# A two-stage transformer block on one core: who writes the 64 duplicated columns of the normalised x in the first chunk

## The chip, the cores and the metric

The kernel runs on one core of a Trainium2 chip. A core has five engines that run side by side, each with its own instruction queue: TensorE (PE in the profile, with its weight loads as PEld), VectorE (DVE), ScalarE (ACT), GpSimd (POOL) and SyncE (SP), which here only starts DMA transfers. An instruction starts when those ahead of it on its engine have started and every semaphore that it waits for has been reached. The metric is the time of one execution in microseconds (us), as the median of several runs.

## The reference, cut to what matters

x has 2048 rows of 576 columns. It is normalised row by row, and the normalised rows feed two branches, whose product is added to x:

```python
xn = _layernorm(x, axis=-1)          # (x - mean) / sqrt(var + 1e-5)
s = _A_ref(xn, A_wqkv, A_wo)         # 32 heads of 18, causal window of 256, softmax, output projection
g = _silu(_B_ref(xn, w_gate, w_up, w_down))   # (sigmoid(xn @ w_gate) * (xn @ w_up)) @ w_down, F = 4608
return x + s * g
```

All tensors are bf16. By far the most work is in the three 576 x 4608 products.

## The kernel before

The rows are worked on in four chunks of 512 (NC = 4, BPC = 4 blocks of 128 rows in each). For each chunk the kernel normalises x, brings it into transposed form (`xnT`, columns of x along the partitions), makes q, k and v, does the windowed attention, the output projection, the gate and up products (instruction names `f1`), their combination `hT`, and the down product (`f2`). All matmuls use 64 rows of the array, two at a time: one on rows 0 to 63 and one on rows 64 to 127. 576 columns are 64 + 4 x 128, so the first 64 columns of x are a block of their own, and both halves of the array need that block. That is why a normalised block `xnr` has 640 columns: columns 64 to 639 hold the 576 normalised values, and columns 0 to 63 are a second copy of the first 64 of them (RD = 64, XW = 640).

The normalisation of block i is built in `build_ln`. For blocks 0, 1 and 3 of the first chunk: two `bn_stats` on VectorE (L545, L547), `bn_aggr` (L549), variance plus epsilon (L551), the power -1/2 on GpSimd (L553), then the normalisation of 576 columns on VectorE (L561, name `ln:ap`), and a copy of 64 columns on VectorE (L565, `ln:dup`). Block 2 has its sums from ScalarE instead (`STATS_ACT = (2,)`): L604 sums x, GpSimd turns that into the negative mean (L605), L606 sums squares, GpSimd makes variance (L607) and the power (L608). Then the same L561 and L565 follow. In the first chunk TensorE transposes the 640 columns of each block in ten pieces of 64 x 64 (L617, `tr`), and ScalarE (blocks 0 to 2) or VectorE (block 3) copies the result from PSUM to `xnT` (L594, `xe`). In later chunks a DMA transposes; there L561 and L565 stay as they are.

Before the first block is ready TensorE has nothing to do, and 106 "warm" matmuls on zeros stand there (L131 with `hT` as input): 86 ahead of the first transposes and 20 behind them. After that come the gate and up products of the first two groups of 128 hidden columns, cut into four parts of 128 rows, so that part i can start as soon as block i is in `xnT` (`NEARLY = 2`, `PARTS`).

The order of the instructions on every engine is not the order of the code. `build_graph` makes a list of operations with their dependencies and an estimated duration (`op(engine, ns, ...)`), `schedule` simulates the engines with those estimates and always takes the operation that can start first, and `emit` writes each engine's list with the semaphore waits. So a changed estimate or a changed engine can move operations on all engines. Small buffers are rings (`Ring`): the statistics have three slots (`NST = 3`), so the statistics of block 3 go where those of block 0 were and wait until their last reader is done; the normalised blocks have two (`NXN = 2`), so block 2 waits for the transposes of block 0.

Of the kernel before, what the change touches and what calls it, by code (L numbers as in the profile page):

```python
# [4 lines left out]
ACTF = mybir.ActivationFunctionType  # L5
ALU = mybir.AluOpType
# [8 lines left out]
RD = 64  # L15
# [59 lines left out]
REM_PRIO = 0.6  # L75
STATS_ACT = (2,)
APPLY_ACT = ()
DUP_ACT = ()
XE_ENG = ("ACT", "ACT", "ACT", "DVE")
NWARM = (43, 10)  # L80
NEARLY = 2
# [25 lines left out]
def act_ns(n):  # L107
    return n / 1.2 + 175.0
# [34 lines left out]
def dve_ns(n, rate=1.0):  # L143
    return n / (0.96 * rate) + 160.0
# [118 lines left out]
class Builder:  # L263
# [17 lines left out]
    def op(self, eng, est, fn, name="", deps=(), prio=3, nbytes=0, odeps=(), acq=None, ni=0):  # L281
        o = Op(eng, est, fn, name, deps, prio, nbytes, odeps, acq)
        o.ni = ni
        assert ni or eng != "PE", name
        o.cidx = len(self.ops)
        self.ops.append(o)
        for d in o.deps:
            d.succs.append(o)
        for d in o.odeps:
            d.succs.append(o)  # L290
        return o
# [237 lines left out]
    def build_ln(self, c):  # L529
        op = self.op  # L530
        xs = c % 2
        war = self.xnT_rel[c - 2] if c >= 2 else []
        for i in range(BPC):
            st = c * BPC + i
            if c and i % 2 == 0:
                self.load_x(c, i)
            pr = 2 if c else LN_PRIO[i]
            o_x, x_in = self.x_dma[st]
            ss, ds = self.r_st.produce()
            on_act = c == 0 and i in STATS_ACT  # L540
            if on_act:
                mean, rs = self.act_stats(x_in, o_x, pr)
                ag = None
            else:
                b1 = op("DVE", 390, lambda e, ss=ss, x_in=x_in: e.bn_stats(self.bnst[:, ss, 0, :], x_in[:, 0:288]),  # L545
                        f"ln:bn1:{st}", deps=[o_x, ds], prio=pr)
                b2 = op("DVE", 390, lambda e, ss=ss, x_in=x_in: e.bn_stats(self.bnst[:, ss, 1, :], x_in[:, 288:576]),  # L547
                        f"ln:bn2:{st}", deps=[o_x, ds], prio=pr)
                ag = op("DVE", 200, lambda e, ss=ss: e.bn_aggr(self.mv[:, ss, :], self.bnst[:, ss, :, :]),  # L549
                        f"ln:ag:{st}", deps=[b1, b2], prio=pr)  # L550
                ve = op("DVE", 140, lambda e, ss=ss: e.tensor_scalar(self.veps[:, ss, :], self.mv[:, ss, 1:2], EPS, None,  # L551
                                                                    ALU.add), f"ln:ve:{st}", deps=[ag], prio=pr)
                rs = op("POOL", 560, lambda e, ss=ss: e.tensor_tensor(self.rstd[:, ss, :], self.veps[:, ss, :],  # L553
                                                                      self.neghalf[:, :], ALU.pow),
                        f"ln:rs:{st}", deps=[ve, self.op_negh], prio=pr)
                mean = self.mv[:, ss, 0:1]
            rstd = self.arstd[:, :] if on_act else self.rstd[:, ss, :]
            sn, dn = self.xn_slot[st] if c else self.r_xn.produce()

            def norm(e, mean=mean, rstd=rstd, x_in=x_in, sn=sn, op0=ALU.add if on_act else ALU.subtract):  # L560
                return e.tensor_scalar(self.xnr[:, sn, RD:XW], x_in, mean, rstd, op0, ALU.mult)  # L561

            def f_dup(e, sn=sn):
                dst, sr = self.xnr[:, sn, 0:RD], self.xnr[:, sn, RD:2 * RD]
                return e.activation(dst, sr, ACTF.Copy) if e is self.nc.scalar else e.tensor_copy(dst, sr)  # L565
            if c == 0 and i in APPLY_ACT:
                nb = op("DVE", 150, lambda e, mean=mean, rstd=rstd, sg=1.0 if on_act else -1.0: e.tensor_scalar(
                    self.nbias[:, :], mean, rstd, sg, ALU.mult, ALU.mult), f"ln:nb:{st}", deps=[rs, ag], prio=pr)
                ap = op("ACT", act_ns(D), lambda e, rstd=rstd, x_in=x_in, sn=sn: e.activation(
                    self.xnr[:, sn, RD:XW], x_in, ACTF.Identity, bias=self.nbias[:, :], scale=rstd), f"ln:ap:{st}", deps=[nb, dn], prio=pr)  # L570
            else:
                ap = op("DVE", 430, norm, f"ln:ap:{st}", deps=[rs, ag, dn], prio=pr)
            dup_act = c == 0 and i in DUP_ACT
            dup = op("ACT" if dup_act else "DVE", act_ns(RD) if dup_act else 180, f_dup, f"ln:dup:{st}", deps=[ap], prio=pr)
            self.ln_dup = dup
            self.r_st.release(ss, ap)
            if c:
                fl = self.flip(self.xnT[:, xs, :, i * P:(i + 1) * P], self.xnr[:, sn, :], f"flip:x:{st}", ("fx", xs, i),
                               deps=[dup, war], prio=2)
                self.r_xn.release(sn, fl)  # L580
                self.op_xnT[c].append(fl)
                continue
            h = self.pool_s.hold()

            def f_tr(eng, h=h, sn=sn):
                return self.transposes(eng, h, lambda r, o: self.xnr[r, sn, o:o + P])
            tr = op("PE", KB * 29.5, f_tr, f"tr:{st}", deps=[ap, dup, self.op_ident, war], prio=0, acq=h, ni=20)
            self.r_xn.release(sn, tr)
            if i == 0:
                self.warm(NWARM[1], None, tr, 80)  # L590

            def f_xe(e, h=h, i=i):
                dst = self.xnT[:, xs, :, i * P:(i + 1) * P].rearrange("p k (t c) -> p t k c", t=2)
                return e.activation(dst, self.tr_src(h), ACTF.Copy) if e is self.nc.scalar else e.tensor_copy(dst, self.tr_src(h))  # L594
            eng = XE_ENG[i]
            xe = op(eng, dve_ns(KB * P, 1.9) if eng == "DVE" else act_ns(KB * P), f_xe, f"xe:{st}", deps=[tr], prio=0)
            h.release(xe)
            self.op_xnT[c].append(xe)
# [765 lines left out]
```

## Time and profile before

| | |
|---|---|
| time, median of 3 runs | 557.19 us (556.58 to 557.23) |
| profiled execution, span | 555.2 us, so about 2.0 us lie around the span |
| TensorE busy | 551.0 us (99%), 8342 matmuls |
| VectorE busy | 323.5 us (58%) |
| ScalarE busy | 271.8 us (49%) |
| GpSimd busy | 209.6 us (38%) |
| granted TensorE clock | 1.0 throughout |
| DMA | 75.87 MB, mean 137 GB/s |

The span is the time from the first to the last instruction of one profiled execution; the times of the runs are a little longer. A row of the timeline gives the start and duration of an instruction (or of several of one kind, merged), the engine, the line, what is written and read, and in square brackets how long the engine stood idle before it and what ended that. A row of a group gives the busy time of all and the mean of one in ns. With TensorE busy for 99% of the span, what matters is whether its queue ever stands still, and for how long.

### The profile page before, as it was taken

How to read it: one execution, taken by the hardware profiler on the slowest of the kernel's cores; microseconds unless marked ns; L12 is line 12 of the kernel's file. 1: busy time of each engine (PE TensorE's matmuls, PEld its weight loads, DVE VectorE, ACT ScalarE, POOL GpSimd, SP SyncE). 2: the span in 40 equal slices, each digit the busy share in tenths (PEclk: the TensorE clock that was granted, in tenths of full speed). 3: DMA queues.
4: the chain of work that ended last, by engine and by line, in shares of the span. 5: the costliest groups of instructions: out<-in, count | busy, mean ns of one | idle time of the engine just before them, and what ended most of it. 6: DMA issues, size and time to landing. Idle time of an engine off the chain costs nothing.

```text
span 555.2 us, 19409 instructions
## 1 busy us (share of the span) xinstructions
PE 551.0 (99%) x8342; PEld 341.3 (61%) x8342; DVE 323.5 (58%) x782; ACT 271.8 (49%) x379; POOL 209.6 (38%) x360
## 2 busy tenths in 40 slices
PE   9999999999999999999999999999999999999998
PEld 7454445777555555567855565447876655445887
DVE  5467564854867555735656567663455657754511
ACT  4246563444465552645265573763265554775021
POOL 5634343563562330564453304742363331700300
PEclk9999999999999999999999999999999999999999
DMA  8899999342377664462126663663013474640001
GB/s 221 241 251 261 250 260 264 89 83 54 77 194 202 179 167 136 126 156 58 33 64 171 211 171 106 182 181 84 14 34 102 119 204 120 171 134 2 20 28 46
DMA packets 141213, 75.87 MB, mean 137 GB/s; under 512 B 43676, under 2 KB 139260, under 8 KB 141128
## 3 DMA queue, kind: packets, MB, share of 16 engines
q1 hardware_dynamic: 133704, 68.71, 46.9%
q0 software_dynamic: 7424, 5.92, 4.1%
q8 instruction: 66, 1.08, 0.8%
q14 instruction: 19, 0.16, 0.1%
HBM read 63.18 MB, written 2.36 MB: 118 GB/s over the span
## 4 chain that ended last, share of the span: by engine, by line
PE 98%; DVE 1%; DMA 0%; issue 0%; ACT 0%
PE ps L131 95%; PE ps L821 3%; DMA x<-in_A_x_dram 0%; DVE small L545 0%; DVE small L547 0%; DVE xnr L561 0%; PE ps L617 0%; DVE xnr L565 0%; DVE small L549 0%; ACT thf L1091 0%; DVE small L551 0%; DVE thf L1093 0%; DVE xf L1096 0%
## 5 line engine op out<-in xcount | busy, mean ns | idle before, releaser
L131 PE MATMUL ps<-xnT,wgs 64*128 64x512 bf16 (+1 forms) x2400 | 283.7, 368 | 0.1
L771 ACT ACTIVATE expr<-ps 128x1024 bf16<-128x1024 f32 (+4 forms) x160 | 155.0, 969 | 86.8 <-PE ps L131 85.0
L131 PEld LDWEIGHTS ps<-xnT,wgs 64*128 64x128 bf16 x2400 | 114.4, 94 | 108.7 <-issue 0.7
L131 PE MATMUL ps<-wd_sb,hT 64*128 64x288 bf16 (+2 forms) x2448 | 152.8, 276 | 0.0
L981 DVE SCALAR_TENSOR_TENSOR hT<-tring,ps 128x512 bf16<-128x512 bf16 x144 | 98.6, 684 | 79.6 <-ACT tring L978 77.5
L978 ACT ACTIVATE tring<-ps 128x512 bf16<-128x512 f32 x144 | 86.2, 598 | 116.5 <-PE ps L131 114.8
L294 POOL DMA_DIRECT2D qk<-qd x160 | 83.3, 527 | 157.7 <-PE ps L131 151.3
L131 PEld LDWEIGHTS ps<-wd_sb,hT 64*128 64x128 bf16 x2448 | 112.8, 94 | 29.5
L784 DVE TENSOR_TENSOR expr<-expr,mask 128x128 bf16<-128x128 bf16 (+2 forms) x240 | 64.7, 297 | 62.6 <-ACT expr L771 60.2
L294 POOL DMA_DIRECT2D oT<-o2T x72 | 36.8, 519 | 109.2 <-DVE ot L852 53.1
L735 POOL TENSOR_SCALAR kx<-kprev,small 128x256 bf16<-128x256 bf16 x64 | 60.1, 949 | 7.1 <-PE ps L131 6.2
L131 PE MATMUL ps<-qk,kx 64*128 64x320 bf16 (+1 forms) x704 | 59.2, 254 | 0.0
L131 PE MATMUL ps<-xnT,wgr 64*128 64x512 bf16 (+1 forms) x300 | 56.0, 367 | 0.0
L131 PEld LDWEIGHTS ps<-qk,kx 64*128 64x128 bf16 x704 | 31.8, 94 | 26.0
L131 PE MATMUL ps<-xnT,wqg 64*128 64x512 bf16 (+1 forms) x320 | 37.7, 355 | 0.0
L656 DVE CAST qd<-ps 128x1024 bf16<-128x1024 f32 (+1 forms) x20 | 22.3, 1116 | 9.3 <-PE ps L131 9.2
L849 DVE STREAM_TRANSPOSE ot<-ps 128x512 f32<-128x512 f32 x32 | 20.2, 687 | 12.0 <-PE ps L821 12.0
L735 DVE TENSOR_SCALAR kx<-qk,small 128x512 bf16<-128x512 bf16 x64 | 21.4, 364 | 7.9 <-PE ps L131 7.8
L131 PEld LDWEIGHTS ps<-xnT,wgr 64*128 64x128 bf16 x300 | 15.0, 94 | 16.5
L857 DVE STREAM_TRANSPOSE o2T<-o 128x512 bf16<-128x512 bf16 x32 | 22.6, 706 | 2.8 <-DMA oT<-o2T 2.5
L131 PEld LDWEIGHTS ps<-xnT,wqg 64*128 64x128 bf16 x320 | 15.1, 94 | 11.4 <-issue 0.4
L718 DVE CAST v_aug<-ps 64x288 bf16<-64x288 f32 x32 | 14.5, 453 | 10.2 <-PE ps L131 9.5
(68 smaller groups left out, 285.3 us busy)
## 6 DMA issues: line engine op xcount, KB each, us to landing
wgs<-in_B_w_gate_dram SPq DMA_DIRECT2D x72, 256.0 KB, 3.4
wgs<-in_B_w_up_dram SPq DMA_DIRECT2D x72, 256.0 KB, 4.0
wd_sb<-in_B_w_down_dram SPq DMA_DIRECT2D x9, 576.0 KB, 5.7
wqg<-in_A_wqkv_dram SPq DMA_DIRECT2D x32, 128.0 KB, 4.1
qk<-qd POOLq DMA_DIRECT2D x100, 36.0 KB, 2.8
wgr<-in_B_w_gate_dram SPq DMA_DIRECT2D x36, 64.0 KB, 3.3
wgr<-in_B_w_up_dram SPq DMA_DIRECT2D x36, 64.0 KB, 3.0
wvo<-in_A_wqkv_dram SPq DMA_DIRECT2D x4, 576.0 KB, 4.4
```

What stands on the lines that cost most here:

```text
L131: res = eng.matmul(outs[i], lhs(ROWS[t], i), rhs(ROWS[t], i), start=start, stop=stop, tile_position=(64 * t, 0))
L294: o = self.op(eng, DMA_ISSUE_NS[eng], lambda e: e.dma_start(dst, src), name, deps, prio, nbytes=nbytes)
L656: return eng.tensor_copy(dst, self.both(h, n))
L718: return eng.tensor_copy(dst, src)
L735: return e.tensor_scalar(self.kx[:, sx, pos:pos + n_ // SW, t, :], src.rearrange("p (s k) -> p s k", k=SW), self.half[:, t:t + 1], None, A ...
L771: return eng.activation(self.expr[:, se, :, lo * SW:NT], self.both(h, NT)[:, :, lo * SW:NT], ACTF.Exp, scale=SM_SCALE)
L784: return eng.tensor_tensor(e_, e_, m_, ALU.mult)
L821: res = eng.matmul(outs[i][p0:p0 + VH, cols], self.v_aug[ROWS[i], o:o + VH], self.expr[ROWS[i], se, t, cols], start=m == 0, stop=m == len( ...
L849: return e.transpose(self.ot1[:, p1, :], self.halves(hp, NT, un)[i])
L857: t2 = op("DVE", dve_ns(NT), lambda e, p2=p2, p3=p3: e.transpose(self.o2T[:, p3, :], self.o2[:, p2, :]), f"ot2:{c}:{pr}:{i}", deps=[on, d3 ...
L978: th = op("ACT", act_ns(NT), lambda e: e.activation(self.tring[:, st, :], bank(h, 0), ACTF.Tanh, scale=0.5), f"th:{c}:{ft}", deps=[pg, dt_ ...
L981: mu = op("DVE", dve_ns(NT), lambda e: e.scalar_tensor_tensor(self.hT[:, ft, :], self.tring[:, st, :], 1.0, bank(h, 1), ALU.add, ALU.mult) ...
```

## The change

In the first chunk the copy of 64 columns (`ln:dup`) goes away on VectorE. GpSimd computes the same 64 values itself, from x with the mean and the factor, as VectorE computes the 576. It no longer depends on the normalisation on VectorE but on the statistics. Since it reads the statistics, their slot is now released by both operations.

```diff
-DUP_ACT = ()
+DUP_POOL = (0, 1, 2, 3)
...
             def f_dup(e, sn=sn):
-                dst, sr = self.xnr[:, sn, 0:RD], self.xnr[:, sn, RD:2 * RD]
-                return e.activation(dst, sr, ACTF.Copy) if e is self.nc.scalar else e.tensor_copy(dst, sr)
+                return e.tensor_copy(self.xnr[:, sn, 0:RD], self.xnr[:, sn, RD:2 * RD])
...
                 ap = op("DVE", 430, norm, f"ln:ap:{st}", deps=[rs, ag, dn], prio=pr)
-            dup_act = c == 0 and i in DUP_ACT
-            dup = op("ACT" if dup_act else "DVE", act_ns(RD) if dup_act else 180, f_dup, f"ln:dup:{st}", deps=[ap], prio=pr)
+            if c == 0 and i in DUP_POOL:
+                def f_dp(e, mean=mean, rstd=rstd, x_in=x_in, sn=sn, op0=ALU.add if on_act else ALU.subtract):
+                    return e.tensor_scalar(self.xnr[:, sn, 0:RD], x_in[:, 0:RD], mean, rstd, op0, ALU.mult)
+                dup = op("POOL", 350, f_dp, f"ln:dup:{st}", deps=[rs, ag, dn], prio=pr)
+            else:
+                dup = op("DVE", 180, f_dup, f"ln:dup:{st}", deps=[ap], prio=pr)
             self.ln_dup = dup
             self.r_st.release(ss, ap)
+            self.r_st.release(ss, dup)
```

## The prediction

> **What bounds the kernel now.** I read the busy shares first, then the waits of TensorE, then the chain that ended last up to 12 us, then the timeline of that stretch.
>
> ```profile
> PE 551.0 (99%) x8342; PEld 341.3 (61%) x8342; DVE 323.5 (58%) x782; ACT 271.8 (49%) x379; POOL 209.6 (38%) x360
> ```
>
> ```profile
> PE ps L131 <- DVE small L463: 1.0, 1, 1.0
> PE ps L821 <- issue: 0.4, 1, 0.4
> ```
>
> TensorE is the bound and hardly waits, so what changes its queue after its first real work lengthens or shortens the kernel by that much, and what doesn't is worth nothing. The change is in the first 10 us; there the chain of work that ended last says:
>
> ```profile
> 7.12 0.19 DVE xnr L565
> 7.32 0.04 issue
> 7.36 0.32 PE ps L617 x10
> 7.68 0.84 PE ps L131 x26
> 8.52 0.15 PE ps L617 x10
> 8.66 1.30 PE ps L131 x45
> 9.97 0.20 PE ps L617 x10
> 10.16 0.11 PE ps L131 x3
> 10.27 0.10 issue
> ```
>
> The copy of block 1 ends just ahead of its transposes. From 7.36 us on the chain is TensorE alone: the transposes of block 2 and 3 (8.34 and 9.84 us by their own rows) stand between matmuls. The timeline has the small steps:
>
> ```profile
> 4.41 0.57 POOL L553 TENSOR_TENSOR small<-small 128x1 f32<-128x1 f32 x1 [2.60 <-DVE small L551]
> ...
> 5.02 0.43 DVE L561 TENSOR_SCALAR xnr<-x,small 128x576 bf16<-128x576 bf16 x1
> 5.17 0.37 POOL L605 TENSOR_SCALAR small<-small 128x1 f32<-128x1 f32 x1 [0.19 <-ACT tring L604]
> ...
> 6.60 0.19 POOL L607 TENSOR_SCALAR small<-small 128x1 f32<-128x1 f32 x1
> ...
> 6.88 0.62 POOL L608 TENSOR_TENSOR small<-small 128x1 f32<-128x1 f32 x1
> ...
> 7.53 0.43 DVE L561 TENSOR_SCALAR xnr<-x,small 128x576 bf16<-128x576 bf16 x1 [0.23 <-POOL small L608]
> ```
>
> GpSimd is no bystander: every mean and factor passes it, and block 2 needs three of its steps in a row (L605, L607, L608). Block 2's copy (7.99, 0.18) ends at 8.17 us and TensorE loads its weights at 8.29: 0.1 us to spare, no more.
>
> **The price of the new operation.** No row has it. Alone, I bound it by rows of GpSimd:
>
> ```profile
> L735 POOL TENSOR_SCALAR kx<-kprev,small x64: 914/933/1187, 16.1 to 484.8; 128x256 bf16<-128x256 bf16 x64
> ```
>
> This is the same kind of instruction, one operation on 256 columns, 0.914 us at the least; L607 has one column in 0.193. Between them 64 columns take 0.193 + 63 x (0.914 - 0.193)/255 = 0.37 us. The floor is a plain GpSimd copy of 256 columns (mean 418 ns), by the same step 0.25; if a second operation costs as much as the first it is 0.193 + 2 x 0.18 = 0.55. I take 0.40, nearest to the L735 row. [...]
>
> It is not alone. It starts with VectorE's normalisation of the same block, on the same factor. What that costs: L605 took 0.37 beside L561 where the same one-column form took 0.19 (L607), 0.17 more; and of two L735 in a row
>
> ```profile
> 255.85 2.10 POOL L735 TENSOR_SCALAR kx<-kprev,small 128x256 bf16<-128x256 bf16 x2
> ```
>
> took 2.10 and not 1.82, 0.28 more, with a VectorE product starting at 256.74, just before the second. At 242.20 two took the plain 1.82 and VectorE paid instead (its L735 0.53 beside them, mean 0.364). So the bounds are 0 and 0.28 for GpSimd, with 0.18 on VectorE where GpSimd goes free. I take 0.28, since VectorE starts first here too. [...]
>
> **The change part by part**, times in us from the span's start.
> - Block 0. The factor is there at 4.98; VectorE normalises 5.02 to 5.45 as before. GpSimd starts at 5.05 (0.06 after its own result, as between its two memsets at 9.85 and 10.84) and ends at 5.05 + 0.40 + 0.28 = 5.73 (the copy ended at 5.66). Only warm matmuls wait.
> - Behind it in GpSimd's queue stands L605: 5.75 to 5.94, not 5.17 to 5.54. ScalarE's squares (L606 and its read-out, 0.87) follow, to 6.84 instead of 6.44, and behind them in ScalarE's queue the copy of block 0 to `xnT`: 7.43 instead of 7.03. The first gate matmuls began at 7.49: just not late.
> - VectorE without the copy is 0.21 earlier: variance of block 1 at 5.75. The statistics of block 3 now wait for GpSimd's end at 5.73 (the ring of three): 0.06, no matter. The factor of block 1 waits for L605: 5.95 to 6.52 (was 6.62). Normalise 6.56 to 6.99; GpSimd 6.58 to 7.26 (copy: 7.30). Transposes at 7.32 to 7.36: no gain. The built order also puts 24 warm matmuls behind the first transposes, not 20, at 0.053 each: TensorE would not be free before 7.33. And the first part's last weights, issued at 4.31, land 3.6 later by the row of that tile: 7.9, met without slack today.
> - Block 2. L607 (6.60 before) stands behind block 1's new operation: 7.28 to 7.47; L608 to 8.15 (was 7.50). Normalise 8.19 to 8.62, GpSimd 8.21 to 8.89. Transposes at 8.95, not 8.34: TensorE stands 0.6.
> - Block 3. The factor is computed behind block 2's operation: 8.91 to 9.46 (was 9.11); normalise to 9.93, GpSimd 9.52 to 10.20, transposes at 10.26. In the new order 34 matmuls stand between the two transposes, 0.74, with the transposes' 0.15 TensorE is there at 9.84: another 0.42. Then 0.15 and 20 matmuls moved behind (0.56): 10.97, where the kernel before was at 10.00.
> - There TensorE stood 0.27 before, for "issue" alone. A late TensorE may find that gone: 0.70 late, or 0.97 if it stays. I take 0.8.
> - VectorE's eight tiny memsets now wait for the last new operation, ahead of its copy of block 3: to 11.24, needed at 11.38 + 0.8. GpSimd's big memsets are 0.4 later; the first transfers that need them are issued at 24.9. SP's first 20 issues keep their order; then one load of q's weights goes behind two gate and up loads (1.1 later, landed 16.9 before), and the first q matmuls, at 19.7, read others. A later TensorE gives all weights more time.
> - After that the built order is the same but for some 180 of 8342 matmuls moved by a few places in chunks 1 to 3; the attention-value runs move by at most 7 instructions. Costed at nothing: TensorE is busy all the way, so there is no slack that takes back 0.8, nor a stall to be saved but one of 0.59 (216.7 us).
>
> Sum: 555.2 + 0.8 = 556.0 for the profiled span, and with the 2.0 around it 558.0; on the median 557.19 + 0.8 = 558.0.
>
> **The rivals.**
> - *Slower by over 0.2% (1.1 us, about what can be told from no change).* Each extra 0.1 us of the new operation comes four times in the chain of GpSimd (blocks 0, 1, 2, 3). With 0.55 in place of 0.40, and the 0.27 not absorbed: 0.97 + 0.60 = 1.6, 558.8. It decides from 0.48 with absorption (0.70 + 4 x 0.08 = 1.02), and 0.44 without. For it: two operations with two factors, where the row has one. Against: the second may ride along. With the like of a stall of 0.59 in moved matmuls the same. 0.37.
> - *The clock falls back.* Pairs of 128 columns step 107 ns up to 6.9 us and 56 ns after 7.36, past a wait of 0.39. If two waits (0.6 and 0.4) undid that, 50 pairs at 107 would add 2.5 us: 560.5. Against it: the 0.39 did no harm. [...] 0.03.
> - *Hidden.* Without contention and at 0.37 block 2 is ready at 8.26, block 3 at 9.3, both before TensorE: 557.1 to 557.3. For it: the undelayed pair at 242.2. 0.13.
> - *Faster by over 0.2%.* It would need both stalls (0.27, 0.59) and more gone; 1.0 at most: 556.2. 0.04.
>
> **How the numbers follow.** The likeliest, contention with about 0.40, has 0.43 and 558.0, in its own range 557.5 to 558.3; with the hidden case that is 0.56 for within 0.2%, the two slower cases make 0.40, faster 0.04. The range leaves out the clock and the gain: 556.8 to 559.1.
>
> **What would show it.** After: L607 at about 7.3 and L608's end near 8.1; the new GpSimd rows 0.5 to 0.7 each beside L561; TensorE idle ahead of the third and fourth transposes, released by POOL; the end of L821 and all else in order. If the new rows are below 0.4, TensorE does not wait and I am wrong to the fast side; above 0.8, to the slow one. Idle TensorE later than 12 us would be another cause.

## The result and the profile after

The changed kernel takes 558.71 us in the median of 5 runs (558.45 to 559.34), the kernel before 556.70 (556.37 to 557.23): 2.0 us slower in the medians, the ratio of the times 1.0033 with a 95% interval of 1.0021 to 1.0045. So it is slower by more than 0.2%. The time lies in the range (556.8 to 559.1), 0.7 above the predicted 558.0; but the case held likeliest, "within 0.2%", did not come. The rival "slower by over 0.2%" did, at 558.71 where it gave 558.8.

The profiled execution has a span of 557.5 us, 2.3 more than before, at a granted clock of 1.0. Its busy shares, in the page's first part:

```profile
PE 550.4 (99%) x8342; PEld 339.6 (61%) x8342; DVE 323.9 (58%) x778; ACT 271.4 (49%) x379; POOL 212.0 (38%) x364
```

The four instructions have gone from VectorE (782 to 778) to GpSimd (360 to 364), and TensorE's work is what it was. The 2.3 us are standstill. The waits of TensorE in the changed kernel (total, times, longest):

```profile
PE ps L621 <- POOL xnr L574: 1.2, 2, 0.7
PE ps L825 <- issue: 1.1, 1, 1.1
PE ps L131 <- DVE small L463: 1.0, 1, 1.0
PE ps L131 <- issue: 0.7, 1, 0.7
PE ps L621 <- DVE small L525: 0.3, 1, 0.3
```

Before, this list had the 1.0 for L463 and one 0.4 for "issue". New are waits of the transposes (L621, the old L617) for the new GpSimd operation (L574), one of 0.7 us for "issue" on the gate and up matmuls (L131), and one for "issue" on the attention-value matmuls (L825, the old L821) that grew from 0.4 to 1.1. The waits at L621 and the 0.7 lie in the first 12 us. The two that make 1.2 are ahead of blocks 0 and 1 (0.59 and 0.66 in the timeline); there TensorE also stood before, for VectorE's copy (0.17 and 0.39 by its weight loads), so not all of it is loss. The 0.3 for L525 is block 3's: tiny memsets on VectorE, which had themselves waited for the GpSimd operation, end last there. The chain that ended last goes through GpSimd there (start, duration):

```profile
5.05 0.74 POOL xnr L574
5.79 0.22 POOL small L609
6.01 0.55 POOL small L553
6.56 0.10 issue
6.67 0.79 POOL xnr L574
7.45 0.14 issue
7.59 0.32 PE ps L621 x10
7.91 0.40 PE ps L131 x8
8.31 0.00 POOLq L1315
8.31 0.04 issue
8.36 0.55 POOL xnr L574
8.90 0.52 POOL small L553
9.43 0.09 issue
9.52 0.75 POOL xnr L574
10.27 0.04 issue
10.32 0.09 DVE small L525 x2
10.41 0.32 PE ps L621 x10
10.73 0.65 PE ps L131 x21
11.38 0.65 issue
12.03 17.99 PE ps L131 x216
```

Before, this chain came to TensorE with the copy of block 1 at 7.36 us and stayed there. Now it goes GpSimd, TensorE, GpSimd, TensorE: the small steps on the statistics (L609, L553, L612) stand in one queue with the four new operations. The step from TensorE back to GpSimd at 8.31 goes by the semaphore that came last; GpSimd's own step ahead, L612, had ended only at 8.25, so its queue was busy until then in any case. The step "0.65 issue" follows at 11.38, with no semaphore on record that TensorE waited for. The weight loads stood at the same place before, for less (first line before, second line after):

```profile
10.37 0.62 PEld L131 LDWEIGHTS ps<-xnT,wgs 64*128 64x128 bf16 x21 [0.27 <-issue]
12.03 0.66 PEld L131 LDWEIGHTS ps<-xnT,wgs 64*128 64x128 bf16 x22 [0.77 <-issue]
```

Matched matmul by matmul with the kernel before, TensorE is 1.68 us behind at 16 us. The transposes of block 1 start 0.23 later (7.59 for 7.36), the first gate matmuls behind them another 0.16, the waits ahead of the transposes of blocks 2 and 3 add 0.34 and 0.46, and the stall near 11.4 us is the rest, about 0.5. The lag then stays at 1.68 until 205 us, is 2.3 to 2.4 behind 216 us, and 2.2 at the end. So there are two places. The second is a run of 192 short matmuls of the attention, the third such run of the kernel. TensorE's timeline there, in the kernel before (the row gives start, duration, and in brackets the idle time ahead):

```profile
214.68 1.56 PE L821 MATMUL ps<-expr,v_aug 64*19 64x320 bf16 x116
216.68 1.05 PE L821 MATMUL ps<-expr,v_aug 64*19 64x64 bf16 x76 [0.43 <-issue]
```

and in the changed kernel:

```profile
215.31 1.62 PE L825 MATMUL ps<-expr,v_aug 64*19 64x320 bf16 x125
218.08 1.02 PE L825 MATMUL ps<-expr,v_aug 64*19 64x128 bf16 x67 [1.15 <-issue]
```

The run is the same and breaks off at nearly the same point, but the break is 0.7 longer. The trace has a DMA queue of kind "instruction", on which TensorE's instructions come in packets of 16 KB (66 of them before, 1.08 MB), by the counts below 256 instructions each (a matmul with its weight load is two; 116 others, nearly all of them waits, stand ahead of this run before and 119 after).

Both stalls lie where a packet begins. In all fourteen profiles of this document, those of the experiments below too, the longest gap of the third run is just ahead of the 6081st or 6082nd instruction on record. In the eleven that have the stall near 11 us, it is just ahead of the 449th or 450th. That is 22 x 256 apart. TensorE goes on 1.25 to 1.5 us after the end of a packet each time, the first one of this queue near 11 us and the 23rd at 216 us, which are 22 apart too. So such an "issue" is a wait for instructions. The sentence on when an instruction starts, ahead of the prediction, leaves this wait out: 0.65 and 1.15 us in the changed kernel, with no semaphore on record that TensorE waited for.

Before, the packet at 216 us began 0.54 us ahead of the run; after, 0.24 us behind the run's start. The third run stands 17 places earlier in TensorE's queue in the new order (5832nd instruction instead of 5849th). Counted from the 449th and the 6081st in steps of 256, the last such boundary ahead of the run is the 5825th (449 + 21 x 256): the run begins 7 instructions behind it, where it was 24. Ahead of the 6081st or 6082nd instruction the fourteen profiles show gaps of 0.3 to 1.7 us.

### The profile page after: what moved, and what is told of

Read it like the earlier page. It is cut to its first block, busy times and chain, and to the rows that moved or that the text cites. A ratio compares the mean times of both kernels' runs of the same rounds, so it can differ in the third digit from the quotient of the medians.

```text
span 557.5 us, 19418 instructions
## 1 busy us (share of the span) xinstructions
PE 550.4 (99%) x8342; PEld 339.6 (61%) x8342; DVE 323.9 (58%) x778; ACT 271.4 (49%) x379; POOL 212.0 (38%) x364
## 3 DMA queue, kind: packets, MB, share of 16 engines
q8 instruction: 66, 1.08, 0.8%
## 4 chain that ended last, share of the span: by engine, by line
PE 97%; POOL 1%; issue 0%; DMA 0%; DVE 0%; ACT 0%; POOLq 0%
PE ps L131 94%; PE ps L825 3%; POOL xnr L574 1%; DMA x<-in_A_x_dram 0%; POOL small L553 0%; PE ps L621 0%; DVE small L545 0%; DVE small L547 0%; ACT thf L1095 0%; DVE thf L1097 0%; DVE xf L1100 0%; POOL small L609 0%; DVE small L549 0%; DVE small L551 0%; DVE small L525 0%
## 5 line engine op out<-in xcount | busy, mean ns | idle before, releaser
L131 PE MATMUL ps<-xnT,wgs 64*128 64x512 bf16 (+1 forms) x2400 | 283.9, 368 | 0.7 <-issue 0.7
L131 PEld LDWEIGHTS ps<-xnT,wgs 64*128 64x128 bf16 x2400 | 113.8, 94 | 109.7 <-issue 1.0
L131 PE MATMUL ps<-wd_sb,hT 64*128 64x288 bf16 (+2 forms) x2448 | 152.8, 276 | 0.0
L131 PEld LDWEIGHTS ps<-wd_sb,hT 64*128 64x128 bf16 x2448 | 112.8, 94 | 29.7
L131 PE MATMUL ps<-qk,kx 64*128 64x320 bf16 (+1 forms) x704 | 59.1, 254 | 0.0
L131 PE MATMUL ps<-xnT,wgr 64*128 64x512 bf16 (+1 forms) x300 | 55.9, 367 | 0.0
L131 PEld LDWEIGHTS ps<-qk,kx 64*128 64x128 bf16 x704 | 31.7, 94 | 26.1
L131 PE MATMUL ps<-xnT,wqg 64*128 64x512 bf16 (+1 forms) x320 | 37.7, 355 | 0.0
L131 PEld LDWEIGHTS ps<-xnT,wgr 64*128 64x128 bf16 x300 | 14.9, 94 | 16.6
L131 PEld LDWEIGHTS ps<-xnT,wqg 64*128 64x128 bf16 x320 | 15.1, 94 | 11.4 <-issue 0.4
```

Of the source, the lines that this page charges most:

```text
L131: res = eng.matmul(outs[i], lhs(ROWS[t], i), rhs(ROWS[t], i), start=start, stop=stop, tile_position=(64 * t, 0))
```

## The experiments

Theory "chain": the new operations delay GpSimd's small steps in the first 10 us, TensorE waits, and that is the loss. Rival "order": the rearranged queues cost it, at the start or at the 216 us stall, whoever writes the 64 columns. The two can add. In the ratios the kernel before was timed on the same chip, with 556.6 to 556.75 in the median.

### Who computes, and in which order

The first kernel keeps the order of before on all engines and only afterwards moves the four operations to GpSimd, each right behind its factor (`rs`). The second keeps the order of the changed kernel and moves them back to VectorE as copies, right behind the normalisation (`ap`).

```diff
 # e1: the scheduled kernel before, then
+    for i, dup, rs, fn, deps in b.to_pool:
+        if i in MOVED:                         # MOVED = (0, 1, 2, 3)
+            b.prog["DVE"].remove(dup)
+            b.prog["POOL"].insert(b.prog["POOL"].index(rs) + 1, dup)
+            dup.eng, dup.fn, dup.deps = "POOL", fn, deps
 # e2: the scheduled changed kernel, then
+    for dup, ap, fn in b.to_dve:
+        b.prog["POOL"].remove(dup)
+        b.prog["DVE"].insert(b.prog["DVE"].index(ap) + 1, dup)
+        dup.eng, dup.fn, dup.deps = "DVE", fn, [ap]
```

> The order of all engines is that of the kernel before; only the four 64-column operations are taken off VectorE after the order is made and put on GpSimd right behind the factor they need, computing from x. Theory 'two places' (the GpSimd operation costs 1.7 us in the first 12 us, the new order costs 0.5 to 0.7 in the instruction stall of TensorE near 216 us): span 1.5 to 1.9 above before, the stall near 216 us at 0.6 as before. Theory 'start alone' (the later stall has nothing to do with the order): +2.0 to +2.3, stall 1.3. Theory 'order alone': no change.

> The reverse: the order of all engines is that of the changed kernel, but the four operations are VectorE copies again, each right behind its normalisation. 'Two places': nothing lost in the first 12 us (within 0.2 of before), TensorE stands 1.2 to 1.4 near 216 us instead of 0.6: span 0.5 to 0.8 above before. 'Start alone': within 0.2 of before. 'Order alone': +2.0.

Measured: GpSimd in the old order 558.28, ratio 1.0026 [1.0015, 1.0037]; copies in the new order 557.59, ratio 1.0014 [1.0006, 1.0023]. Both cost, about 1.5 and 0.8 us, which make 2.4 where both together cost 2.0. In the profile of e1, taken in the shortest of its eight runs (557.48), the lag at 16 us is 1.34, with the waits for GpSimd and a stall of 0.8 ("issue"), while at 216 us the run goes through with no gap over 0.35, which is less than before the change:

```profile
216.04 2.77 PE L828 MATMUL ps<-expr,v_aug 64*19 64x320 bf16 x192
```

In the profile of e2 the lag at the start is only 0.36, and the long break at 216 us is there with VectorE copying:

```profile
213.97 1.63 PE L828 MATMUL ps<-expr,v_aug 64*19 64x320 bf16 x126
216.77 1.02 PE L828 MATMUL ps<-expr,v_aug 64*19 64x128 bf16 x66 [1.17 <-issue]
```

So the first place belongs mostly to the engine that computes, the second to the order. Neither theory alone.

### Which blocks

The same edit as e1 for a part of the blocks: block 3 alone (e6), blocks 0 and 1 (e7).

```diff
-MOVED = (0, 1, 2, 3)
+MOVED = (3,)       # e6; (0, 1) in e7
```

> The order of the kernel before; only block 3's operation is on GpSimd, blocks 0 to 2 are copied by VectorE. Nothing on GpSimd is queued behind it in the chain. Theory 'the chain' (the cost is that GpSimd's small steps for blocks 1 and 2 stand behind the operations of blocks 0 and 1): within 0.2 of before, the transposes of block 3 0.1 to 0.2 later. Theory 'each block pays its own': +0.3 to 0.4, a quarter of the 1.3 to 1.5 that all four cost in this order.

> The order of the kernel before; blocks 0 and 1 on GpSimd, blocks 2 and 3 copied by VectorE. 'The chain': the last small step of block 2 ends near 8.24 as with all four (7.50 before), TensorE loses 1.0 to 1.4 in the first 16 us, and the time is that of all four, +1.2 to 1.6. 'Each block pays its own': +0.6 to 0.8.

Block 3 alone costs nothing: 556.71, ratio 1.0001 [0.9993, 1.0009]. Blocks 0 and 1 cost 1.2 us: 557.81, ratio 1.0018 [1.0009, 1.0027], most of e1's 1.5. GpSimd's timeline of e7 shows why, with blocks 2 and 3 still copied by VectorE:

```profile
5.11 0.74 POOL L582 TENSOR_SCALAR xnr<-x,small 128x64 bf16<-128x64 bf16 x1
5.83 0.24 POOL L612 TENSOR_SCALAR small<-small 128x1 f32<-128x1 f32 x1
6.04 0.57 POOL L555 TENSOR_TENSOR small<-small 128x1 f32<-128x1 f32 x1
6.72 0.78 POOL L582 TENSOR_SCALAR xnr<-x,small 128x64 bf16<-128x64 bf16 x1
7.48 0.19 POOL L614 TENSOR_SCALAR small<-small 128x1 f32<-128x1 f32 x1
7.75 0.56 POOL L615 TENSOR_TENSOR small<-small 128x1 f32<-128x1 f32 x1
```

L612, L614 and L615 are the three steps of block 2 (L605, L607, L608 before). Each of the first two waits out one of the new operations, and L615 ends at 8.31 instead of 7.50. With block 3 alone moved it ended at 7.54. The operation costs through what is queued behind it, not where its own result is needed.

### What the operation itself costs

Two ways to make it cheaper or dearer in place. In e3 each also waits for VectorE's normalisation of its block, so that it runs without it. In e5 blocks 0, 1 and 3 add the mean, as block 2 does with its negative mean, instead of subtracting it (their 64 columns are then not normalised by the right value, at the same amount of work).

```diff
 # e3: the scheduled changed kernel, then
+    for dup, ap in b.later:
+        dup.deps.append(ap)
 # e5
-                def f_dp(e, mean=mean, rstd=rstd, x_in=x_in, sn=sn, op0=ALU.add if on_act else ALU.subtract):
+                def f_dp(e, mean=mean, rstd=rstd, x_in=x_in, sn=sn, op0=ALU.add):
```

> The changed kernel, with each GpSimd operation made to wait for VectorE's normalisation of the same block, so that the two never run side by side. [...] With contention the span is within 0.5 of the changed kernel.

> The changed kernel, in which GpSimd adds the mean in blocks 0, 1 and 3 too instead of subtracting it (as it does for block 2, where the mean is stored negative): the sign of the mean is left out in 64 columns, all else is the same. Theory 'the subtraction is dear' (alone 0.40 with an add against 0.59 with a subtraction): the four operations all take 0.54 to 0.58 beside VectorE instead of 0.74 to 0.78, TensorE's third transposes come 0.3 to 0.45 earlier, and the time falls by 0.5 to 1.0 against the changed kernel. Theory 'block 2 is quick because its factor comes from another place': the durations stay 0.74 to 0.78 and the time too.

The durations are by line, min/median/max in ns, of the changed kernel:

```profile
L574 POOL TENSOR_SCALAR xnr<-x,small x4: 547/738/776, 5.1 to 9.5; 128x64 bf16<-128x64 bf16 x4
```

of e3:

```profile
L575 POOL TENSOR_SCALAR xnr<-x,small x4: 400/590/595, 5.6 to 11.2; 128x64 bf16<-128x64 bf16 x4
```

and of e5:

```profile
L574 POOL TENSOR_SCALAR xnr<-x,small x4: 536/544/547, 5.0 to 9.1; 128x64 bf16<-128x64 bf16 x4
```

The minimum in the first two is block 2, the only one that adds. So the operation takes 0.40 us with an addition and 0.59 with a subtraction when it runs behind the normalisation, and 0.15 more beside it in either form; e5 shows that it is the addition and not the block that makes the difference. VectorE is not slowed by it: in the first chunk of the changed kernel L561 takes 0.41 to 0.43 us, and 0.43 before.

The times went another way. e3 has 560.27, ratio 1.0061 [1.0047, 1.0074], 1.6 above the changed kernel: waiting for the normalisation costs more than the 0.15 that it saves, four times in the chain. But this is not all of it, and the expectation did not have the rest. TensorE waits 1.51, 1.05 and 0.56 us ahead of its first three sets of transposes here, and then its clock falls: the granted clock is 0.52 from 10.6 to 12 us and 0.50 from 12 to 14, and pairs of 128 columns step 107 ns from 10.67 to 14.06 us instead of 56. At 10.6 us TensorE is 1.2 behind the changed kernel; the slow stretch adds about as much, and 0.7 comes back because the gap near 11 us is 0.17 here for 0.86. e5 has 558.71, ratio 1.0033 [1.0021, 1.0045], the changed kernel's time to the hundredth, where a gain of 0.5 to 1.0 was expected. Its transposes of blocks 2 and 3 are 0.46 and 0.66 us earlier (8.56 for 9.02, 9.72 for 10.38). Its waits for "issue" take that back:

```profile
PE ps L825 <- issue: 1.5, 1, 1.5
PE ps L131 <- issue: 0.9, 1, 0.9
```

TensorE reaches the place of the first stall 0.6 us earlier and leaves it 0.4 earlier (11.65 for 12.03); the rest of the gain goes at 216 us (1.5 for 1.1). The packet ahead of the first stall ends at 10.36 here and at 10.53 in the changed kernel, and TensorE goes on 1.29 and 1.50 later. So a quicker chain alone does not bring the time back.

### The order at 216 us

In e4 the changed kernel's planner is asked for the third run a little later, which puts it 27 instructions behind the boundary. In e8 the kernel before has four more warm matmuls (two more pairs) behind the first transposes and is planned anew, which puts its third run 12 behind.

```diff
 # e4, the changed kernel
-RUN_NEED = (1.1, 1.0, 1.0, 1.0, 1.0, 1.0, 1.1, 1.0)
+RUN_NEED = (1.1, 1.0, 1.05, 1.0, 1.0, 1.0, 1.1, 1.0)
 # e8, the kernel before
-NWARM = (43, 10)
+NWARM = (43, 12)
```

> The changed kernel, with the planner's need for fetched instructions ahead of the third attention-value run raised from 1.0 to 1.05, which puts ten more matmuls in front of that run (it begins at TensorE's instruction place 2986 instead of 2976; before 2983). If the place of the run against the fetch grid sets the stall near 216 us, it falls from 1.3 to 0.6 or less, and the span by 0.6 to 0.9 against the changed kernel. If the late start of the kernel sets it, it stays at 1.3 and the time is that of the changed kernel.

> The kernel before, VectorE copies and all, with four more warm matmuls behind the first transposes (24 instead of 20). It moves every later place in TensorE's queue: the third attention-value run begins 12 instructions behind a boundary of 256 instead of 24 (7 in the changed kernel, 4 with its order and copies). If the place behind that boundary sets the stall near 216 us, it is 1.0 to 1.3 here, and the kernel 0.4 to 0.8 slower without any GpSimd operation. If the stall comes with the moved matmuls of the changed order and not with the place, it stays at 0.6 and the time within 0.2.

e4: 557.99, ratio 1.0017 [1.0008, 1.0026], 0.72 us below the changed kernel, and the break is as before the change:

```profile
215.87 1.56 PE L825 MATMUL ps<-expr,v_aug 64*19 64x320 bf16 x115
217.86 1.06 PE L825 MATMUL ps<-expr,v_aug 64*19 64x64 bf16 x77 [0.43 <-issue]
```

Some of that is at the start, though: its stall near 11 us was a gap of 0.32 between two matmuls in the profiled execution, and 0.86 in the changed kernel, so e4 does not isolate the run wholly. e8 got the long break without any change of engine, as the place foretold:

```profile
214.33 1.60 PE L821 MATMUL ps<-expr,v_aug 64*19 64x320 bf16 x122
217.10 1.03 PE L821 MATMUL ps<-expr,v_aug 64*19 64x128 bf16 x70 [1.17 <-issue]
```

But its time, 561.51, ratio 1.0080 [1.0066, 1.0094], is 4.9 us up where 0.4 to 0.8 was expected. It has another break of that size in the fifth run (1.07 idle at 340 us, though that run stands 32 behind its boundary; the break is at a boundary again, the 9921st instruction, whose packet began 0.41 behind the run's start), one of 0.85 at 10 us, and some 2.2 us at the end, where the new order lets the last load of x wait for a store. So it confirms the place for the third run, and also that the place is not the whole rule. The kernel before says the same: its fourth run stands 24 behind a boundary as its third does, its packet begins 0.78 ahead of it, and no gap in it is over 0.12.

Over all kernels the third run's stall (the gap between two matmuls) sorts by where the packet stands: 1.4 to 1.7 us when the run begins 4 to 12 instructions behind the boundary (the changed kernel, e2, e3, e5, e8; the packet begins 0.24 to 0.68 us behind the run's start in them), and 0.3 to 0.8 when it begins 24 to 54 behind (the kernel before and the other eight; the packet 0.45 to 0.78 us ahead of the run's start). One profile each.

### The stall near 11 us, without moving anything else

This stall lies at the same place of TensorE's queue in eleven of the fourteen kernels, ahead of its 449th or 450th instruction. To move it against the work, 8 or 14 warm matmuls (16 or 28 instructions) were put ahead of the first transposes of the kernel before, with the order otherwise kept (e9, e11), and the same with the operations on GpSimd as in e1 (e10, e12).

```diff
+    pe = b.prog["PE"]
+    at = next(k for k, o in enumerate(pe) if o.name.startswith("tr:"))
+    pe[at:at] = [pe[at - 1]] * 4        # 8 matmuls; * 7 makes 14
```

> The kernel before, VectorE copies and its order on every engine, with eight more warm matmuls (16 instructions) ahead of the first transposes, put in after the order is made. Everything behind them stands 16 instructions later in TensorE's queue: the third attention-value run begins 40 behind a boundary of 256 instead of 24. If that distance sets when the next 16 KB packet of instructions starts (0.3 to 0.7 after the run's start at 4 to 12, 0.5 to 0.7 before it at 24 to 27), it starts 1 us or more before it here, the stall near 216 us (0.6 before) is gone, and the time is 0.3 to 0.7 below before. If the stall belongs to that place of the work, it stays at 0.6 and the time within 0.2.

> The same with all four 64-column operations on GpSimd behind their factors, in the order of the kernel before. With the later stall gone in both, the difference between this kernel and the one with copies is what the GpSimd operations cost in the first 16 us: 1.0 to 1.5 if it is their chain, whatever the stall of TensorE at its place 228 does. If the cost came from the two instruction stalls alone, under 0.5.

> As the first, with 14 more warm matmuls (28 instructions): the run begins 52 behind the boundary. No stall near 216 us; the warm matmuls now take 0.75 more and some of it stands in front of block 0's transposes and behind them: equal to the first or up to 0.4 slower.

> The order of the kernel before with 14 more warm matmuls ahead of the first transposes, as in the third kernel of the last set, and all four operations on GpSimd behind their factors. With copies at the same places the packet of instructions that TensorE stood for at 10 us began at 6.2, and the lag of TensorE at 16 us was 4.1. If the GpSimd operations hold TensorE by their own lateness, the third and fourth transposes start near 9.0 and 10.5 here too and the lag is 4.8 to 5.3 with no stall over 0.3 between 10.7 and 13: 0.7 to 1.2 above the same kernel with copies. If what they cost is the late packet alone, an early packet brings the lag to 4.1 to 4.4 and the time to that of the copies.

| kernel | median | ratio, 95% |
|---|---|---|
| e9, 8 more, copies | 557.17 | 1.0007 [0.9990, 1.0025] |
| e10, 8 more, GpSimd | 557.39 | 1.0006 [0.9992, 1.0021] |
| e11, 14 more, copies | 559.01 | 1.0054 [1.0040, 1.0068] |
| e12, 14 more, GpSimd | 559.03 | 1.0042 [1.0029, 1.0056] |

Most of what was expected missed. GpSimd against copies costs 0.2 us in the median with 8 more warm matmuls (by the spread of the runs -0.7 to 0.8), not 1.0 to 1.5, and nothing with 14 (-1.2 to 0.5 by five runs each). e9 did not gain by leaving its stall; it got a wait for a weight load instead, seen in its waits:

```profile
PE ps L131 <- DMA wgr<-in_B_w_up_dram: 0.5, 1, 0.5
```

And the 14 cost 2.3 us either way, more than their own work. With copies the transposes of blocks 2 and 3 are as late as GpSimd makes them (8.94 and 10.41 in e11, with a wait of 0.5 for a weight load that ends at 8.17). But at 16 us e11 is only 0.3 behind the kernel before and 1.4 at 550 us, so most of what its profile shows is lost later. In the profiles e12 is 0.41 behind e11 at 16 us, between the two expectations. The profile of e10 goes against its median: it was taken in the longest of the eleven runs (558.40), and there TensorE is 1.30 behind e9 at 16 us, as expected, with a stall of 1.17 ("issue"). That the GpSimd chain is hidden where something else holds TensorE in these 10 us would fit the medians, but it is argued, not shown. In the order of before and after the operations cost 1.1 us (the changed kernel against e2) to 1.5 (e1).

No kernel tried was faster than the one before.

## Why the prediction was right and wrong

- **The price of the operation: right in sum, wrong in its parts.** 0.40 alone and 0.28 for contention were to make 0.68; measured are 0.59 and 0.15, 0.74 together (0.74, 0.78 and 0.74 for blocks 0, 1 and 3). The "second operation" was the open end of the working, with 0.55 as the upper bound; it is not the second operation that makes it but the subtraction. For block 2, which adds, 0.40 was exact and the sum too high (0.55).
- **The chain of GpSimd: right.** L605's successor ran from 5.78 (forecast 5.75), L607's from 7.42 (7.28), L608's ended at 8.25 (8.15), the transposes of blocks 2 and 3 began at 9.02 (8.95) and 10.38 (10.26), and the 20 matmuls behind the last were done at 11.14 (10.97). "Transposes at 7.32 to 7.36: no gain" was 0.23 short, block 1's operation ending at 7.45 instead of 7.26, through two operations 0.06 and 0.10 dearer. The other reason given there did not hold: the 24 warm matmuls were done at 6.93, not at 7.33.
- **The step that failed first: "A late TensorE may find that gone ... I take 0.8."** The 0.27 of idle time for "issue" was taken as slack that a late TensorE would use up. It was no slack but a wait for instructions: with a packet that began later too (9.17 us instead of 7.85, with its end at 10.53 instead of 9.07), TensorE went on at 12.03 instead of 10.37. In the sum, 0.17 was taken off the chain's 0.97, to 0.8. The runs put 0.54 on top of 1.14, to 1.68.
- **The step that failed second: "After that ... Costed at nothing."** The queue was known to be rearranged, and the 0.59 break at 216.7 us was named, but only as a stall that might be saved. The text held the runs to move "by at most 7 instructions"; the third moved by 17 (10 matmuls with their weight loads, less 3 waits; it is 7 where a matmul with its weight load counts as one), and its break grew by 0.7. e2 shows that the order alone does this, and e4 that it goes when the run moves back. "Idle TensorE later than 12 us would be another cause" was the sign named for it.
- **The rivals.** "Slower by over 0.2%" came, and it names the right places: the dearer operation, the 0.27 not absorbed, and "the like of a stall of 0.59 in moved matmuls". That its 558.8 fits is luck. It gave 0.60 to the dearer operation, and the chain was only 0.17 later than forecast (1.14 for 0.97), since less contention (0.15 for 0.28) made up for most of the price; the two stalls brought the rest. It is luck too that the range held, since it was not drawn for two stalls that grow. The clock did not fall back: it is 1.0 in the profile, and pairs of 128 columns still step 56 ns behind the new waits. e3 shows that this rival was nearer than its chance of 0.03 says: there the clock fell with no wait over 1.51 us ahead of it. That the 0.39 in the kernel before did no harm, the reason given against it, says nothing of waits of 1.51, 1.05 and 0.56. "Hidden" fell with the price of the operation.

**What stays open.** What decides when the early packet starts. It began at 7.6 to 8.4 us in the kernel before, e2, e6 and e8 (6.2 and 6.6 in e11 and e9), which have copies in blocks 0 to 2, and at 8.6 to 9.5 in the changed kernel, e1, e4, e5, e7 and e10 (8.5 in e12, 10.7 in e3), which have GpSimd in blocks 0 and 1 at least. Each pair that differs in the engine alone, in one profile each, has it later with GpSimd: the kernel before and e1 (7.85, 9.10), e2 and the changed kernel (8.32, 9.17), e9 and e10 (6.56, 9.00), e11 and e12 (6.17, 8.48). So the GpSimd operations go with a later packet; by what link is open. In the changed kernel and e1 it began about 0.1 us behind the start of block 2's transposes, but in e4 and e10 ahead of it, and in e7, where VectorE copies block 2, 0.42 behind. So the split of the 1.68 us between the chain (at least the 1.03 of waits seen) and the late packet is read from one trace's waits, not shown by an experiment: e5 and e10 say that the two are not independent. Why the packet in the fifth run of e8 came late is open too.

## What to carry to other kernels

An operation moved to an engine with time to spare is charged for what it pushes back in that engine's queue: here two operations of 0.74 and 0.78 us on GpSimd between 5 and 7.5 us, with another block's small steps queued behind them, cost 1.2 us (e7), and the same operation on the last block cost nothing (e6). A short idle time that the profile gives to "issue" was not slack to be used up here: it grew from 0.27 to 0.77 us by the weight loads while TensorE came later; look at the instruction packets around it. And where a planner writes the order, even a local change can move runs of very short matmuls against the packets (here by 17 places of the queue, 200 us later, where a break of 0.43 became 1.15), so compare the places in the queue before an order is costed at nothing.

## What the hardware showed that was not expected

- On GpSimd, subtract-and-multiply on 128 x 64 bf16 values took 0.59 us and add-and-multiply 0.40, with per-row factors in both (e3), and 0.74 to 0.78 against 0.54 to 0.55 beside VectorE's normalisation.
- TensorE's instructions came in packets of 16 KB, 256 instructions by the distance of the two stalls (5632 instructions and 22 packets). A run of 192 short matmuls (2.5 us when nothing breaks it, as the fourth run) went on for 1.2 to 1.4 us in the third run, and then stood still until 1.25 to 1.5 us after the end of the next packet, by "issue" alone. For that run, 4 to 12 instructions behind a boundary went with 1.4 to 1.7 us, and 24 to 54 with 0.3 to 0.8; for other runs the same place gave no break, so look at when the packet begins.
- The granted TensorE clock fell to 0.5 for 3.4 us in e3, behind three waits of 1.51, 1.05 and 0.56 us with work between them.
- A few more idle-time matmuls were not free: 14 in a stretch where TensorE waits anyway made the kernel 2.3 to 3.0 us slower (e11 by its ratio 3.0), of which its profile has 0.3 in the first 16 us.
